# Soft-capped attention and a soft mixture of experts: tanh of three-tile chunks a step ahead of the exp of six tiles, two score buffers, and second-layer loads in pairs of blocks

## The chip, the core and the metric

The kernel runs on one core of a Trainium2 chip. The core has a matrix engine (TensorE, PE), two engines for elementwise work (VectorE, DVE, and ScalarE, ACT, which has the activation functions), a slower general engine (GpSimd, POOL) and a queue engine (SyncE, SP) that mostly starts DMA transfers. Each engine takes its instructions in order, and waits between engines are semaphores. Matmul results go to PSUM, eight banks of 512 fp32 columns on 128 partitions. The metric is the device time of one execution in microseconds (us); lower is better.

## What is computed

Attention has 8 batches, 12 heads, 448 positions and head size 64. The scores are capped by a tanh before the softmax. Its output, reordered to 3584 tokens of 768 features, is the input of a mixture of 8 experts with 4 slots each: every slot is a softmax-weighted mean over all tokens, goes through its expert's two layers, and every token gets back a softmax-weighted mean of the slots.

```python
scores = scale * q @ k.T
scores = cap * tanh(scores / cap)              # cap = 30
attn = softmax(scores, axis=-1)
x = (attn @ v) reordered to [3584, 768]
logits = x @ phi                               # [3584, 32]
d = softmax(logits, axis=0)                    # over tokens
slot_input = (d.T @ x).reshape(8, 4, 768)
for e in range(8):
    slot_out[e] = relu(slot_input[e] @ w1[e]) @ w2[e]     # 768 -> 1024 -> 768
out = softmax(logits, axis=1) @ slot_out       # over slots
```

## The kernel before, in words

**Attention.** Two heads make a pair and two pairs a quad, so there are 24 quads and 48 pairs. A tile is 64 keys of both heads of a pair (128 partitions) by 448 queries; a pair has 7 tiles, and there are 336 in all. The main loop (L402) runs over 84 chunks of four tiles. `qk_chunk` (L215) makes a chunk's transposed scores, two matmuls a tile, in the one score buffer of four PSUM banks. `tanh_chunk` (L227) reads it and writes bf16 to SBUF, which frees the score buffer; `exp_chunk` (L232) runs in place on what tanh has just written. `pv_tile` (L235) multiplies the tile of the chunk before with v, and carries a column of ones in v (so `VW` is 130), by which the row sums of the softmax come out of the same matmul. Two banks (`pv0`, `pv1`) hold the four query groups of a pair. At the last tile DVE takes the reciprocal of the sums and multiplies (L254, L255) into `xq`.

**What runs beside it.** q, k and v come in by SP, a quad at a time; DVE casts q and k (`cast`, L180), PE transposes them through PSUM (`transp`, L188), and DVE copies the result back (L194). POOL casts v into a block layout (`vcast`, L199). For each pair `x_transp` (L263) transposes the attention output, for each quad `logits` (L272) adds its part of the logits, and for each batch `e_exp` (L286) exponentiates them into E, `slot_sums` (L313) adds up the weighted tokens with the sum of E as a seventh column block (by a matrix of ones), and `e_transp` (L290) and `e_sums` (L305) prepare the second softmax. Most of these pass through `psT`, two PSUM banks. The weights are cast in flight by DMAs that POOL starts (L102, L106): all of w1 and the first `R2` = 28 of the 64 blocks of w2 to SBUF, and the rest as bf16 to a scratch in DRAM.

The order is written by hand. `at(j, slot, ...)` puts a piece of work beside chunk `j` in slot "a" or "b", and the loop emits tanh, PV tiles, slot "a", the next scores, slot "b" and exp. Waits come only from data and buffer reuse.

**The tail.** After the last exp come the last PV, transposes, logits, E and slot sums (L416 to L428), with junk matmuls (`busy`) between them. The slot inputs are divided by the sum (L445, L446). The blocks of w2 in the scratch are loaded by SP into the SBUF space that the attention buffers leave, four blocks a DMA (L439); each load waits for the buffers under it. `layer1` (L450) runs four times (two groups of four experts, two halves of 512 features), `h_transp` transposes, and `layer2` (L478) goes through the 64 blocks, both halves of the output columns (384 each) four blocks at a time. The results are cast to `so` (L499, L500), and 28 output tiles follow: two matmuls, a scaling on DVE or ACT by turns (L518, L520), and a store of 384 KB by SP (L521).

## Time and profile before

| | |
|---|---|
| median of 4 runs | 340.54 us (337.99 to 346.36) |
| the profiled execution | 339.12 us, of which 337.3 are the span of the profile |
| first tanh, end of the last exp | 8.08 us, 285.09 us |
| busy: ACT, PE, DVE, POOL | 86%, 75%, 48%, 26% |
| granted PE clock, mean | 0.949 |
| DMA in the span | 76.84 MB, 228 GB/s |

The profile gives each instruction's start and length and what ended the idle time before it. A group's row shows its line, engine, result and sources, shapes and count, then its busy time, the mean of one in ns, and the idle time in front of it. In the windows view a row gives PE, PE's weight loads, DVE, ACT and POOL busy, each with its number of instructions in brackets, then PE's clock (1.00 is full), DMA share and GB/s. In the timeline some matmul records are merged, so that "x28" is one row with the length of all, and a release is named after "<-". "PEld" is PE loading weights, "q" behind an engine's name its queue.

### The profile page before, as it was taken

What the parts mean: (1) busy time and instruction counts of PE and PEld (TensorE: products, weight loads), DVE (VectorE), ACT (ScalarE), POOL (GpSimd) and SP (SyncE); (2) the same over time, 40 slices, a digit from 0 to 9 for tenths busy, and PEclk for the clock granted to TensorE, in tenths of its full rate; (3) what the DMA queues carried; (4) which work ended last, traced back from release to release, by engine and by line L of the source; (5) the groups of instructions that cost most, each with busy time, mean ns of one, the idle gap of its engine ahead of it and who ended that gap; (6) DMA issues with size and microseconds to landing.
All of it is one profiled execution on the core that took longest, in us unless ns stands there. A gap on an engine that the chain in (4) does not pass through costs nothing.

```text
span 337.3 us, 7890 instructions
## 1 busy us (share of the span) xinstructions
PE 252.9 (75%) x3398; PEld 180.8 (54%) x3398; DVE 161.6 (48%) x414; ACT 289.8 (86%) x194; POOL 88.6 (26%) x106
## 2 busy tenths in 40 slices
PE   7668778778687787776787777878877877896670
PEld 6446556555465565564665555556654655553220
DVE  6733545355455453563555354633745433316541
ACT  1999999999999999999999999999999997105450
POOL 3630442145124322540342244313404300000000
PEclk9997997999999899999999999997999999999755
DMA  8977778977987899599779999999899920885997
GB/s 272 255 156 221 177 208 194 221 191 202 188 239 180 174 264 237 172 217 209 204 195 198 273 272 235 244 276 279 192 237 240 230 94 2 315 343 219 398 397 294
DMA packets 40740, 76.84 MB, mean 228 GB/s; under 512 B 3201, under 2 KB 29825, under 8 KB 40705
## 3 DMA queue, kind: packets, MB, share of 16 engines
q1 hardware_dynamic: 24656, 50.67, 43.8%
q0 software_dynamic: 15760, 25.22, 42.8%
q8 instruction: 26, 0.43, 0.5%
q10 hardware_dynamic: 288, 0.46, 0.4%
q14 instruction: 10, 0.07, 0.1%
HBM read 90.54 MB, written 18.09 MB: 322 GB/s over the span
## 4 chain that ended last, share of the span: by engine, by line
ACT 75%; PE 8%; DMA 6%; SPq 3%; DVE 3%; issue 3%; DVEq 0%; ACTq 0%
ACT ex L233 37%; ACT ex L230 37%; DMA w2t<-w2d 4%; SPq L521 3%; PE pv L245 3%; PE sc L224 2%; DMA out_dram<-ob 1%; DMA qraw<-in_q_dram 1%; PE op L514 1%; DVE xq L255 1%; DVE ob L518 1%; ACT E L288 0%; PE xps L267 0%; DVE qT L194 0%; PE slps L321 0%
## 5 line engine op out<-in xcount | busy, mean ns | idle before, releaser
L233 ACT ACTIVATE ex<-ex 128x1792 bf16<-128x1792 bf16 x84 | 142.5, 1696 | 2.4
L230 ACT ACTIVATE ex<-sc 128x1792 bf16<-128x1792 f32 x84 | 138.4, 1647 | 5.7 <-PE sc L224 5.7
L245 PE MATMUL pv<-vbd,ex 128*128 128x130 bf16 x1344 | 101.5, 227 | 28.4 <-ACT ex L233 27.5
L245 PEld LDWEIGHTS <-ex 128*128 128x128 bf16 x1344 | 81.3, 101 | 54.3 <-ACT ex L233 40.2
L224 PE MATMUL sc<-qT,kT 64*64 64x448 bf16 x672 | 71.4, 358 | 31.8 <-ACT ex L230 26.8
L202 POOL CAST vbd<-vraw 64x896 bf16<-64x896 f32 x23 | 21.6, 939 | 174.5 <-PE pv L245 144.9
L224 PEld LDWEIGHTS <-kT 64*64 64x64 bf16 x672 | 35.1, 105 | 44.1 <-issue 27.6
L269 DVE COPY xT<-xps 128x512 bf16<-128x512 bf16 x48 | 20.3, 423 | 56.9 <-PE xps L267 56.8
L255 DVE TENSOR_TENSOR xq<-pv,rec 128x256 bf16<-128x256 f32 x96 | 40.8, 425 | 3.3
L254 DVE RECIPROCAL rec<-pv 128x4 f32<-128x4 f32 x96 | 17.0, 177 | 39.0 <-PE pv L245 39.0
L203 POOL CAST vbd<-vraw 64x896 bf16<-64x896 f32 x23 | 30.8, 1339 | 1.3
L194 DVE COPY qT<-qps 128x896 bf16<-128x896 bf16 x23 | 14.4, 625 | 27.1 <-PE qps L192 27.1
L520 ACT ACTIVATE ob<-op,winv 128x768 f32<-128x768 f32 x14 | 12.5, 901 | 11.3 <-DMA out_dram<-ob 8.5
L514 PE MATMUL op<-so,ET 128*128 128x384 bf16 x56 | 16.8, 400 | 5.7 <-DVE ob L518 3.8
L267 PE MATMUL xps<-ident,xq 128*128 128x128 bf16 x192 | 19.2, 223 | 0.6 <-DVE xq L255 0.6
L518 DVE TENSOR_SCALAR ob<-op,winv 128x768 f32<-128x768 f32 x14 | 14.2, 1017 | 9.8 <-PE op L514 7.4
L102 POOL DMA_DIRECT2D w1b<-in_moe_w_dram x24 | 16.9, 705 | 0.0
L182 DVE CAST qbf<-qraw 128x896 bf16<-128x896 f32 x22 | 14.6, 665 | 0.0
L514 PEld LDWEIGHTS <-ET 128*128 128x128 bf16 x56 | 5.9, 108 | 15.5 <-issue 14.2
L194 DVE COPY kT<-kps 128x896 bf16<-128x896 bf16 x23 | 14.2, 617 | 0.0
L192 PE MATMUL kps<-ident,kbf 128*128 128x128 bf16 x161 | 12.9, 220 | 1.2 <-DVE kbf L182 0.9
L267 PEld LDWEIGHTS <-xq 128*128 128x128 bf16 x192 | 13.1, 100 | 0.9 <-DVE xq L255 0.9
(70 smaller groups left out, 174.8 us busy)
## 6 DMA issues: line engine op xcount, KB each, us to landing
w1b<-in_moe_w_dram POOLq DMA_DIRECT2D x24, 512.0 KB, 8.4
out_dram<-ob SPq DMA_DIRECT2D x28, 384.0 KB, 3.9
vraw<-in_v_dram SPq DMA_DIRECT2D x23, 448.0 KB, 7.3
qraw<-in_q_dram SPq DMA_DIRECT2D x22, 448.0 KB, 3.7
kraw<-in_k_dram SPq DMA_DIRECT2D x22, 448.0 KB, 4.8
w2d<-in_moe_w_dram POOLq DMA_DIRECT2D x9, 768.0 KB, 10.9
w2t<-w2d SPq DMA_DIRECT2D x9, 768.0 KB, 8.0
w2b<-in_moe_w_dram POOLq DMA_DIRECT2D x7, 768.0 KB, 11.4
```

The lines of the kernel that those rows point to most:

```text
L194: dve.tensor_copy(t, ps)
L202: pool.tensor_copy(t[0:HP, :, :, 0:DH], raw[0:HP])
L203: pool.tensor_copy(t[HP:P, :, :, DH + 1:VW - 1], raw[HP:P])
L224: pe.matmul(sc[cs, u, 0:S], qkT["k", Q][r, c, cs], qkT["q", Q][r, :, cs], start=True, stop=True)
L230: act.activation(ex, scores.pop(j)[:, :, 0:S], ACT.Tanh, scale=qk_scale / cap)
L233: act.activation(exs[j], exs[j], ACT.Exp, scale=cap)
L245: pe.matmul(pvs[pr][g // 2][:, g % 2, :], exs[j][:, u, GOFF[g]:GOFF[g] + P], vbds[Q % 2][:, h, c, :], start=(c == 0 and g % 2 == 0), stop= ...
L255: dve.tensor_tensor(xq[Q][:, 2 * s:2 * s + 2, h * P:(h + 1) * P] .rearrange("p g (i d) -> p g i d", i=2), pv[:, :, :, 0:DH], rec.to_broadc ...
L267: pe.transpose(ps[:, g, :], xq[Q][:, g, h * P:(h + 1) * P], ident)
L269: dve.tensor_copy(t, ps)
L514: pe.matmul(op[:, half, 0:HD], et_tile(bb, c), so[half], start=True, stop=True)
L518: dve.tensor_scalar_mul(ob, op[:, :, 0:HD], winv[:, bb, c:c + 1])
```

## The change

The number of tiles for an exp goes from four to six (`CH`), and a chunk of scores becomes three tiles (`CS`) in one of two score buffers. A step of the main loop, of which there are 56, emits tanh of its two half chunks and then exp of the six tiles of the step before; the exp buffers go from three to four. PV runs two steps behind, a pair at a time, in two passes of two query groups (`pv_pass`), each in the one bank of `psV`, with the next scores between them. `psT` has one bank. Four slots ("a" to "d") and one in front ("0") take the other work; one step in seven has no pair and gets 12 junk matmuls. V's cast has its own slots.

At the start, the casts' access pattern gets another dimension, the first copy of kT is made in two parts, and the second half's k goes through `psV`. The sum of E is made by `e_norm` from the copy of E that `e_rep` makes on POOL, and the division moves into the Relu of layer 1, as the scale `rz`.

In the tail, exp of the last chunk is in two parts, the PSUM banks form one pool of seven, and the last pair's transposes, logits and E go in halves. `R2` is 24, the scratch is loaded two blocks a DMA, layer 2 makes all of its first half of columns before the second, and the first halves of five output tiles are made and stored while the second half runs.

```diff
-CH = 4
+CH = 6
+CS = 3
...
-    R2 = 28
+    R2 = 24
...
-    psT = ctx.enter_context(tc.tile_pool(name="psT", bufs=2, space=PSUM))
+    psT = ctx.enter_context(tc.tile_pool(name="psT", bufs=1, space=PSUM))
...
+    ldv = att.enter_context(tc.tile_pool(name="ldv", bufs=1))
+    qk = att.enter_context(tc.tile_pool(name="qk", bufs=2))
     vb = att.enter_context(tc.tile_pool(name="vb", bufs=1))
+    exps = att.enter_context(tc.tile_pool(name="exps", bufs=4))
+    xs = att.enter_context(tc.tile_pool(name="xs", bufs=4))
+    attp = ExitStack()
+    psS = attp.enter_context(tc.tile_pool(name="psS", bufs=2, space=PSUM))
+    psV = attp.enter_context(tc.tile_pool(name="psV", bufs=1, space=PSUM))
...
-                casts[nm, 0][:, :, h * HP:(h + 1) * HP],
-                raws[nm, 0][:, h, :].rearrange("p (c d) -> p c d", d=DH))
+                casts[nm, 0][:, :, h * HP:(h + 1) * HP]
+                .rearrange("p c (a d) -> p a c d", a=2),
+                raws[nm, 0][:, h, :].rearrange("p (c a d) -> p a c d", a=2, d=DH // 2))
...
-            ps = psT.tile([P, NT, P], BF16, name=nm + "ps", tag="T")
+            ps = (psT if nm == "q" else psV).tile(
+                [P, NT, P], BF16, name=nm + "ps", tag="T" if nm == "q" else "pv")
             r = slice(h * HP, h * HP + HP)
             for c in range(NT):
                 pe.transpose(ps[r, c, :], casts[nm, 0][:, c, r], ident)
-            dve.tensor_copy(qkT[nm, 0][r], ps[r])
+            cuts = (0, 2, NT) if (nm, h) == ("k", 0) else (0, NT)
+            for c0, c1 in zip(cuts, cuts[1:]):
+                dve.tensor_copy(qkT[nm, 0][r, c0:c1, :], ps[r, c0:c1, :])
...
+    def qk_chunk(i):
+        sc = psS.tile([P, CS, 512], F32, name="sc", tag="sc")
+        scores[i] = sc
+        for u in range(CS):
+            pr, c = divmod(i * CS + u, NT)
             Q, h = divmod(pr, 2)
             r = slice(h * HP, h * HP + HP)
+            for n in range(2):
+                cs = slice(n * HP, n * HP + HP)
                 pe.matmul(sc[cs, u, 0:S], qkT["k", Q][r, c, cs],
                           qkT["q", Q][r, :, cs], start=True, stop=True)
+    def tanh_chunk(i):
+        j, half = divmod(i, CH // CS)
+        if half == 0:
+            exs[j] = exps.tile([P, CH, S], BF16, name="ex", tag="ex")
+        act.activation(exs[j][:, half * CS:half * CS + CS, :],
+                       scores.pop(i)[:, :, 0:S], ACT.Tanh, scale=qk_scale / cap)
+    def exp_part(j, u0, u1):
+        act.activation(exs[j][:, u0:u1, :], exs[j][:, u0:u1, :], ACT.Exp, scale=cap)
     def exp_chunk(j):
+        exp_part(j, 0, CH)
+    def pv_tiles(pr, half, c0, c1, home=None):
         Q, h = divmod(pr, 2)
+        if c0 == 0:
+            if h == 0 and half == 0:
                 xq[Q] = xs.tile([P, NG, 2 * P], BF16, name="xq", tag="xq")
+            pvs[pr, half] = psV.tile([P, 2, VW], F32, name="pv", tag="pv") \
+                if home is None else home
+        for c in range(c0, c1):
+            j, u = divmod(pr * NT + c, CH)
+            for n in range(2):
+                g = 2 * half + n
+                pe.matmul(pvs[pr, half][:, n, 0:VW],
+                          exs[j][:, u, GOFF[g]:GOFF[g] + P],
+                          vbds[Q % 2][:, h, c, :],
+                          start=(c == 0 and n == 0), stop=(c == NT - 1),
+                          skip_group_check=True)
+    def norm(pr, half):
+        Q, h = divmod(pr, 2)
+        pv = pvs.pop((pr, half))[:, :, 0:VW].rearrange("p g (i w) -> p g i w", i=2)
+        rec = xs.tile([P, 2, 2, 1], F32, name="rec", tag="rec", bufs=4)
+        dve.reciprocal(rec, pv[:, :, :, DH:DH + 1])
+        dve.tensor_tensor(
+            xq[Q][:, 2 * half:2 * half + 2, h * P:(h + 1) * P]
+            .rearrange("p g (i d) -> p g i d", i=2),
+            pv[:, :, :, 0:DH],
+            rec.to_broadcast([P, 2, 2, DH]), op=ALU.mult)
+    def pv_pass(pr, half):
+        pv_tiles(pr, half, 0, NT)
+        norm(pr, half)
...
+    def e_rep(b):
+        e4s[b] = consts.tile([P, NG, 4 * NS], BF16, name="e4", tag="e4", bufs=1)
+        pool.tensor_copy(e4s[b].rearrange("p g (a s) -> p g a s", a=4),
+                         es[b].unsqueeze(2).to_broadcast([P, NG, 4, NS]))
+    def e_norm(b):
+        ps = psT.tile([P, 1], F32, name="zps", tag="T")
+        for g in range(NG):
+            pe.matmul(ps, e4s[b][:, g, :], ones[:, 0:1], start=(g == 0), stop=(g == NG - 1))
+        if b == 0:
+            dve.tensor_copy(zacc, ps)
+        else:
+            dve.tensor_tensor(zacc, ps, zacc, op=ALU.add)
+        if b == B - 1:
+            dve.reciprocal(rz, zacc)
...
+    def slot_mms(b, ps, gs, jts=None):
+        for g in gs:
+            for jt in range(NJ):
+                pe.matmul(ps[:, jt, :],
+                          xq[b * NQB + jt // 2][:, g, (jt % 2) * P:(jt % 2 + 1) * P],
+                          es[b][:, g, :], start=(g == 0 and jt == 0), stop=(g == NG - 1),
+                          skip_group_check=True)
...
+    def spare(n):
+        busy(n, psV.tile([P, 2, VW], F32, name="junk", tag="pv")[:, 0, 0:P])
+    PER = 2 * NQB * NT // CH
+    assert PER == 7 and NQB == 3
+    def quad_in(Q, cast_k, cast_q, k_in, q_in, v_in):
         if 0 < Q < NQ:
             at(*cast_k, cast, "k", Q)
             at(*cast_q, cast, "q", Q)
             at(*k_in, transp, "k", Q)
             at(*q_in, transp, "q", Q)
+            at(*v_in, vcast, Q)
+    for b in range(B):
+        j = b * PER
+        quad_in(3 * b + 1, (j - 1, "d"), (j, "a"), (j, "b"), (j, "c"), (j + 2, "c"))
+        quad_in(3 * b + 2, (j + 1, "c"), (j + 1, "d"), (j + 2, "b"), (j + 2, "c"),
+                (j + 5, "c"))
+        quad_in(3 * b + 3, (j + 3, "d"), (j + 4, "c"), (j + 5, "b"), (j + 5, "c"),
+                (j + 7, "c"))
+        p = 6 * b
+        at(j + 2, "a", spare, 12)
+        at(j + 4, "a", x_transp, p)
+        at(j + 5, "a", x_transp, p + 1)
+        at(j + 6, "a", x_transp, p + 2)
+        at(j + 5, "d", logits, 3 * b)
+        if b < B - 1:
+            at(j + 7, "a", x_transp, p + 3)
+            at(j + 8, "a", x_transp, p + 4)
+            at(j + 7, "d", logits, 3 * b + 1)
+            at(j + 9, "a", x_transp, p + 5)
+            at(j + 9, "d", logits, 3 * b + 2)
+            at(j + 11, "0", e_exp, b)
+            at(j + 11, "d", slot_sums, b)
+            at(j + 12, "d", e_transp, b)
+            at(j + 13, "d", e_norm, b)
+            if b % 2:
+                at(j + 14, "d", e_sums, b // 2)
...
-        at(2 + n * (NCH - 8) // nw, "b", *job)
+        at(1 + n * (NCH - 5) // nw, "b", *job)
...
+    busy(33)
     init_vbd()
     first_half(0)
     qk_chunk(0)
     first_half(1)
+    qk_chunk(1)
+    at(1, "b", vcast, 0)
+    at(3, "b", dve.memset, hpad, 0.0)
     pool.dma_start(out=phib, in_=moe_phi.rearrange("(jt ji) s -> ji jt s", ji=P))
+    def pair_at(j):
+        pr = (j + 1) * CH // NT - 1
+        return pr if pr >= 0 and (pr + 1) * NT > j * CH else None
     for j in range(NCH):
+        run(j, "0")
+        tanh_chunk(2 * j)
+        tanh_chunk(2 * j + 1)
+        if j != 1:
+            exp_chunk(max(j - 1, 0))
+        pr = pair_at(j - 2)
+        if pr is not None:
+            pv_pass(pr, 0)
         run(j, "a")
         if j + 1 < NCH:
+            qk_chunk(2 * j + 2)
         run(j, "b")
+        if pr is not None:
+            pv_pass(pr, 1)
+        run(j, "c")
+        if j + 1 < NCH:
+            qk_chunk(2 * j + 3)
+        run(j, "d")
...
+    exp_part(NCH - 1, 0, CL)
+    exp_part(NCH - 1, CL, CH)
+    attp.close()
+    mid = ExitStack()
+    big = mid.enter_context(tc.tile_pool(name="big", bufs=7, space=PSUM, reuse_waits="tile"))
+    def bank(shape, dt=F32, name="bank"):
+        return big.tile(shape, dt, name=name, tag="b")
+    junk = bank([P, P], name="junk")
+    pv2 = [bank([P, 2, VW], name=f"pvl{half}") for half in range(2)]
+    x_transp(last - 2)
+    for half in range(2):
+        pv = bank([P, 2, VW], name=f"pvm{half}")
+        pv_tiles(last - 1, half, 0, NT, pv)
+        norm(last - 1, half)
+    logits(NQ - 2, bank([P, NG, NS], name="lpl"))
+    for half in range(2):
+        pv_tiles(last, half, 0, NT - CL, pv2[half])
+    x_transp(last - 1)
+    busy(3)
+    for half in range(2):
+        pv_tiles(last, half, NT - CL, NT)
+        norm(last, half)
+    busy(5)
+    xl = xs.tile([P, NG, P], BF16, name="xT", tag="xT", bufs=2)
+    halves = [range(0, 2), range(2, 4)]
+    Q, bl = NQ - 1, B - 1
+    lg, el = lgs.pop(bl), consts.tile([P, NG, NS], BF16, name="E", tag="E", bufs=2)
+    es[bl] = el
+    sl_ps = bank([P, NJ, NS], name="slpl")
+    for s, gs in enumerate(halves):
+        hs = slice(2 * s, 2 * s + 2)
+        ps = bank([P, 2, P], BF16, name="xpl")
+        for g in gs:
+            pe.transpose(ps[:, g - 2 * s, :], xq[Q][:, g, P:2 * P], ident)
+        act.copy(xl[:, hs, :], ps)
+        busy(3)
+    for s, gs in enumerate(halves):
+        hs = slice(2 * s, 2 * s + 2)
+        ps = bank([P, 2, NS], name="lpl")
+        for g in gs:
+            pe.matmul(ps[:, g - 2 * s, :], xTs[2 * Q][:, g, :], phib[:, NJ - 2, :],
+                      start=True, stop=False)
+            pe.matmul(ps[:, g - 2 * s, :], xl[:, g, :], phib[:, NJ - 1, :],
+                      start=False, stop=True)
+        dve.tensor_tensor(lg[:, hs, :], ps, lg[:, hs, :], op=ALU.add)
+        act.activation(el[:, hs, :], lg[:, hs, :], ACT.Exp)
+    busy(5)
+    for gs in halves:
+        slot_mms(bl, sl_ps, gs)
+    for s in range(2):
+        js = slice(3 * s, 3 * s + 3)
+        dve.tensor_tensor(slT[:, js, :], sl_ps[:, js, :], slacc[:, js, :], op=ALU.add)
+    e_rep(bl)
...
-    for n0 in range(R2, len(blocks), 4):
-        t = tl.tile([P, 4, D], BF16, name=f"w2t{n0}")
-        sp.dma_start(out=t, in_=w2d[(n0 - R2) // 4])
+    for n0 in range(R2, len(blocks), 2):
+        t = tl.tile([P, 2, D], BF16, name=f"w2t{n0}")
+        sp.dma_start(out=t, in_=w2d[(n0 - R2) // 4][:, (n0 - R2) % 4:(n0 - R2) % 4 + 2, :])
...
-            act.activation(hbs[i][:, 0:512], hp, ACT.Relu)
+            act.activation(hbs[i][:, 0:512], hp, ACT.Relu, scale=rz)
         else:
-            dve.tensor_scalar_max(hbs[i][:, 512:1024], hp, 0.0)
+            dve.tensor_scalar(hbs[i][:, 512:1024], hp, rz, 0.0, ALU.mult, ALU.max)
...
+    def layer2(n0, half):
+        for n in range(n0, n0 + 4):
+            i, ft, gg = blocks[n]
+            pe.matmul(so_ps[half][32 * gg:32 * gg + NS, :],
+                      hpad[:, 4 * i + gg, ft, :],
+                      w2_block(n)[:, half * HD:(half + 1) * HD],
+                      start=(n0 == 0), stop=(n0 == len(blocks) - 4))
...
+    layer1(0, 0, e_norm)
...
+    def half_tile(n, half, home, eng):
+        if half == 0:
+            obs[n] = wts.tile([P, 2, HD], F32, name="ob", tag="w1", bufs=E)
+        bb, c = divmod(n, NT)
+        pe.matmul(home, et_tile(bb, c), so[half], start=True, stop=True)
+        if eng == "dve":
+            dve.tensor_scalar_mul(obs[n][:, half, :], home, winv[:, bb, c:c + 1])
+        else:
+            act.mul(obs[n][:, half, :], home, winv[:, bb, c:c + 1])
+        store(n, half, half + 1)
...
+    NH = 5
+    so = [wts.tile([P, HD], BF16, name=f"so{half}", tag="w1", bufs=E) for half in range(2)]
+    n2 = len(blocks)
+    for n0 in range(0, n2, 4):
+        if n0 == n2 // 2:
             h_transp(1)
+        layer2(n0, 0)
     act.copy(so[0], so_ps[0])
+    done = 0
+    for n0 in range(0, n2, 4):
+        layer2(n0, 1)
+        if n0 >= 8 and n0 % 8 == 0 and done < NH:
+            half_tile(done, 0, bank([P, HD], name="op0"),
+                      "act" if done % 2 else "dve")
+            done += 1
...
+        if n == NH + 2:
             e_transp(B - 1)
+        if n == NH + 4:
             e_sums(B // 2 - 1)
         op = fin.tile([P, 2, 512], F32, name="op", tag="op")
+        if n < NH:
+            half_tile(n, 1, op[:, 0, 0:HD], "act" if n % 2 else "dve")
+            continue
```

## The prediction

> **What bounds it now.** I read the page's chain and costliest groups first, then ScalarE's (ACT's) timeline, then TensorE (PE) and VectorE (DVE) between two chunks, then the DMA view of the last 67 us.
>
> ```profile
> span 337.3 us, 7890 instructions
> ...
> ACT 75%; PE 8%; DMA 6%; SPq 3%; DVE 3%; issue 3%; DVEq 0%; ACTq 0%
> ...
> L233 ACT ACTIVATE ex<-ex 128x1792 bf16<-128x1792 bf16 x84 | 142.5, 1696 | 2.4
> L230 ACT ACTIVATE ex<-sc 128x1792 bf16<-128x1792 f32 x84 | 138.4, 1647 | 5.7 <-PE sc L224 5.7
> ```
>
> Tanh (L230) and exp (L233) are three quarters of the chain. Of the 5.7 us idle before tanh, 5.14 is the start (first tanh at 8.08), so attention is ACT-bound from 8.08 to 285.09, the end of the last exp. After that: 52.2 us.
>
> The ACT timeline (start, length) shows where two instructions touch:
>
> ```profile
> 49.50 1.70 ACT L233 ACTIVATE ex<-ex 128x1792 bf16<-128x1792 bf16 x1
> 51.11 1.65 ACT L230 ACTIVATE ex<-sc 128x1792 bf16<-128x1792 f32 x1
> 52.78 1.70 ACT L233 ACTIVATE ex<-ex 128x1792 bf16<-128x1792 bf16 x1
> 54.39 1.65 ACT L230 ACTIVATE ex<-sc 128x1792 bf16<-128x1792 f32 x1
> 55.93 0.30 ACT L288 ACTIVATE E<-lg 128x128 bf16<-128x128 f32 x1
> 56.13 1.69 ACT L233 ACTIVATE ex<-ex 128x1792 bf16<-128x1792 bf16 x1
> 57.99 1.66 ACT L230 ACTIVATE ex<-sc 128x1792 bf16<-128x1792 f32 x1 [0.17 <-PE sc L224]
> ```
>
> A tanh starts 1.61 after an exp of 1.70: 0.09 of overlap. The exp that reads what the tanh just wrote starts 1.67 after it, with none, and 0.02 lost. Where E (which reads something else) stands between, tanh and E overlap by 0.11. So the dependence costs about 0.11 a pair, and a pair takes 3.28.
>
> **ScalarE in attention.** The new loop has 56 steps of tanh, tanh (three tiles each) and the exp of six tiles of the step before. The count is unchanged (168 instructions), but only the first exp and the tail's read what the previous instruction wrote. Lengths: between casts of 384 elements (479 ns, L499) and tanh (1647) the slope is 0.83 ns an element; between E (300 ns at 128) and exp (1696) it is 0.84. So tanh of 1344: 1647 - 448 x 0.83 = 1275; exp of 2688: 1696 + 896 x 0.84 = 2448. Step: 2 x 1.275 + 2.448 - 3 x 0.093 = 4.72. 56 x 4.72 = 264.3, plus 0.2 for the first exp and the split last exp: 264.5, against 84 x 3.28 = 275.5. **Gain 11.0.** The Trainium skill, "ScalarE: Activation LUTs", section "What ACT_TABLE_LOAD costs", gives 186 ns + 0.833 a column for any activation with immediates, and 93 ns of overlap back to back. By it a step is 3 x 0.186 + 5376 x 0.000833 - 0.279 = 4.76, and the gain only 275.5 - 266.6 - 0.2 = 8.7. The rows show two fixed costs, not one (0.15 for tanh from PSUM, 0.19 for exp from SBUF), and the change trades exps for tanhs; I take the rows. The eight E cost 0.2 each as before.
>
> **The start.** Casts of 448 take 0.61 (L167); those of 896 with one more loop dimension in their pattern take 0.61 too (L182). The new pattern has that dimension: about 0.38 each, so q and k are ready 0.4 earlier. The kT copy (0.62 for 896) is cut, the first part 256 long (0.28), and the chunk is 6 matmuls, not 8. First tanh near 7.25: **gain 0.8**. If the pattern doesn't help: 0.4. The second tanh waits behind the second half's transposes on PE (about 8.5, when the first ends): nothing.
>
> **What TensorE and VectorE must now hold.** PSUM goes to two score buffers of three banks, and psT and psV fall to one bank. New waits: the second PV half waits for the first's normalization (reciprocal, multiply); every transpose, logit and slot sum waits for the copy of the last user of psT. Behind each of them, in PE's order, stand the next scores that ACT wants.
>
> ```profile
> 99.13 0.94 PE L224 MATMUL sc<-qT,kT 64*64 64x448 bf16 x8 [0.56 <-ACT ex L230]
> 100.01 1.94 PE L245 MATMUL pv<-vbd,ex 128*128 128x130 bf16 x28
> 101.78 0.39 PE L267 MATMUL xps<-ident,xq 128*128 128x128 bf16 x4
> 101.87 0.18 DVE L254 RECIPROCAL rec<-pv 128x4 f32<-128x4 f32 x1 [1.75 <-PE pv L245]
> 102.09 0.42 DVE L255 TENSOR_TENSOR xq<-pv,rec 128x256 bf16<-128x256 f32 x1
> 103.10 0.56 PE L192 MATMUL kps<-ident,kbf 128*128 128x128 bf16 x7
> 103.84 0.62 DVE L194 COPY kT<-kps 128x896 bf16<-128x896 bf16 x1
> ```
>
> PE a batch (7 steps, 33.0 us): 6 pairs x 1.94, 14 half chunks x 0.70, 6 x 0.56, 6 x 0.39, 3 logits x 0.35, slots 0.75, E's transposes, sums and 12 spare matmuls 1.5: 30.3, or 92%. These rows contain each group's drain (28 weight loads of PV take 1.6), so the true need is 25 to 30. A step with both transposes, logits and PV needs 5.2 with drains, over 4.72; the light steps (3.3 without transposes, 2.5 to 3.7 without PV) give it back. Its hand-overs: a normalization takes 0.75 after the half, covered by the 0.70 of scores placed between; a qT copy (0.62) before the logits uncovers about 0.5 behind the last scores of the step. Walking it from tanh's start: first scores end at 2.0 to 2.8, wanted at 4.72; second at 4.7 to 5.4, wanted at 5.9. The next step starts late, and in the one after a heavy one the slack falls to 0 to 0.5. With ex in four buffers, tanh also waits for the first tiles of the previous step's second PV half (at 3.5 to 4.4, wanted by 4.72). So the bound from below is 0, from above 1 us a batch, 8 in all. I take **2.5 lost**, nearer the lower end, since the group rows overstate PE and a late step is made good within two.
>
> The skill's "TensorE: Matmul & The Clock Gate", section "A second HAM failure mode: psum-queue depth-cycling", says that PE idling briefly between groups that cycle through PSUM can make its clock fall back again and again. That speaks against one bank for psT. The trace has such falls:
>
> ```profile
> 30.00:32.00 2.00, 2.00 (x19) 1.31 (x14) 0.18 (x1) 2.00 (x2) 0.00 (x0) 0.50 0.42 72
> ...
> 30.69 3.02 PE L245 MATMUL pv<-vbd,ex 128*128 128x130 bf16 x28
> ```
>
> At clock 0.50 the 28 PV matmuls take 3.02, not 1.94; ACT lost 0.24 after it and 0.17 at 58 us (row above). By windows the clock means 0.95 to 1.00 from 62 to 267, some 14 us at half speed in all attention. The same four falls would each take 1.7 us of PE's work, mostly within slack: they are in the 2.5. By the rule at its worst, the last rival below.
>
> **Queues and edits at nothing.** V casts move to later slots on POOL: a V cast may start when PE leaves the buffer of two quads earlier and is wanted one quad (11.0 us) later; casts 2.3, landing 7.3 (longest 10.1): cover about 8 us, and without it PV would wait for the excess. K and q loads on SP keep their order; they land in 3.3 to 7.6, wanted 8 us later. Weight loads keep their number (40; POOL issue 0.7) and end by about 245. The copy of E to e4 on POOL (0.61) has a step of time. The ones matmuls of the slot sums (4 a batch) become four of the E sums; the scale by 1/z enters the Relu. DVE is 48% busy.
>
> **The tail.**
>
> ```profile
> 286.25 4.90 SPq L439 DMA_DIRECT2D w2t<-w2d  x7
> 304.03 0.51 PE L482 MATMUL so_ps<-w2t,hpad 128*32 128x384 bf16 x8 [1.02 <-DMA w2t<-w2d]
> ...
> GB/s 301 125 21 0 0 0 0 0 0 10 117 374 334 330 422 435 408 411 388 92 0 0 273 396 398 394 398 396 402 394 404 393 400 398 394 396 396 392 347 13
> ...
> out_dram<-ob SPq DMA_DIRECT2D x28, 384.0 KB, 3.9
> ```
>
> Let T be the last exp's end (285.09). Seven w2t loads (5.5 MB) wait for the last PV and land at T+18.9; layer 2 ends behind them; output then flows from T+21.9 at about 395 GB/s for 28 us (11 MB). Both are DMA-bound. Now ten groups come back (R2 = 24: 0.8 MB more) but in 20 pieces, the first eight of which wait only for the last loads, casts and earlier PV, and land before T. Twelve (4.7 MB) wait for the last PV, at about T+1.9 because PV of two pairs queues in front (PE behind by 0.7 to 1). 4.7 MB at 388 GB/s is 12.2: landing at T+16. The slot chain (layer 1 at T+5.2, was 6.35) is hidden by it. Half 0 of layer 2 ends at T+16.1, its cast and first half store put output on at T+18.4: five halves (1 MB, 2.5 us) flow while half 1 (64 matmuls, 2.7) runs. Half 1, cast, scale: the rest flows from T+22.0, a gap of 1.1, for 25.7, and ends at T+47.7 where it was T+50.2. **Gain 2.5**; none if the loads slip by 2.5, 4 if the gap closes. The extra SP issues (0.37) hide under transfers of 0.5.
>
> **Sum.** 337.3 - 11.0 - 0.8 + 2.5 - 2.5 = 325.5. The profiled execution took 339.12, 1.8 over its span: 327.3. That run is 1.4 under the median of the four (340.54), so I put the median at **328.0**.
>
> **Rivals.** (a) The loop is as costed, PE loses nothing: 325 to 326, and 323 with a tail gain of 4. Chance 0.25. (b) As forecast, 326 to 331: 0.43. (c) PSUM hand-overs cost 1 us a batch or more and the tail gives nothing: 328 + 5.5 + 2 = 332 to 336. For it: heavy steps over 4.72; against: each is followed by light ones. 0.19. (d) The overlap isn't got, because a tanh that waits on a semaphore starts afresh; without it for the two tanhs a step is 4.91 and attention 275: 338 to 339.5. Against it: the tanh at 51.11 waits on PE too and overlaps. 0.06. (e) Slower: the single psT and psV banks make PE stall into the slow clock for good. PE's 25 us a batch at half clock is 50, 7.1 a step, 2.4 over ACT's 4.72; six slow steps (40 us, where before had 14) take all the gain, ten give 350. 0.07.
>
> Faster by over 1% 0.87, within 1% (about what a measurement can tell from no change) 0.06, slower 0.07. Range 322.5 to 335: (a), (b) and most of (c).
>
> **What would show it.** ACT: exp rows of 2448, tanh 1275, step 4.72, every neighbour overlapping 0.09. Idle before tanh from PE in steps 1 and 2 of each seven, 2 to 3 us in all. Last exp's end near 275. Last w2t landing 16 us after it, output on by 18.4, the end 49.7 after it. Wrong if PE's clock is low for long stretches, if idle before tanh passes 8, or if POOL waits for V loads and PV for POOL.

## The result, and the profile after

The kernel after the change takes 338.32 us (median; 333.11 to 351.18) where the kernel before takes 340.3 in the same comparison. Executions of one kernel scatter, so the ratio, 0.989 with a 95% interval of 0.986 to 0.991, is taken over those within 1.5% of each kernel's fastest (means 336.1 and 339.9 us), and the profiled execution of the kernel after lies just above that bound. It is 1% faster, not the 3.7% that was forecast, and 338.3 lies outside the range. The profiled execution took 338.42 us, 336.7 of it the span: 11.2 us more than the forecast span (325.5), and these have to be found.

These are rows of the page of the kernel after, in the page's order: the span, the granted clock in 40 slices of 8.4 us, the chain that ended last, and the groups of tanh (L243) and exp (L247).

```profile
span 336.7 us, 8116 instructions
...
PEclk9855999699959999999799959999999699989855
...
ACT 47%; PE 24%; DMA 16%; DVE 8%; issue 2%; SPq 1%; DVEq 0%; ACTq 0%
...
L243 ACT ACTIVATE ex<-sc 128x1344 bf16<-128x1344 f32 x112 | 145.6, 1408 | 14.9 <-PE sc L236 12.0
L247 ACT ACTIVATE ex<-ex 128x2688 bf16<-128x2688 bf16 (+1 forms) x57 | 143.7, 2526 | 0.0
```

ScalarE has fallen from 75% of the chain to 47%; PE, DMA and DVE took its place. In front of tanh ScalarE is idle for 14.9 us, where it was 5.7. Of that, 4.74 is the start (first tanh at 7.68), and 10.1 are stalls inside attention. The last exp ends at 283.56 (forecast 275.8), and the rest takes 53.1 us (forecast 49.7). So 7.8 of the 11.2 us are lost in attention and 3.4 behind it.

The stalls lie in few places: 5.5 us before 36 us, then two each near 61, 96 and 263 us. Ahead of all but the first two (1.61 and 0.23, before 19 us) VectorE waits for a load: 6.76 for k at 21.02, then for q 3.06 at 56.27, 3.00 at 91.30 and 2.01 at 258.22. A fifth wait, 1.41 at 191.51, stalls nothing. This is the timeline of the stall at 96 (start, length; in brackets the idle time before, and what ended it):

```profile
87.69 0.62 DVE L194 CAST kbf<-kraw 128x896 bf16<-128x896 f32 x1
...
88.65 2.55 ACT L243 ACTIVATE ex<-sc 128x1344 bf16<-128x1344 f32 x2
90.07 0.75 PE L236 MATMUL sc<-qT,kT 64*64 64x448 bf16 x6 [1.28 <-ACT ex L243]
90.99 2.54 ACT L247 ACTIVATE ex<-ex 128x2688 bf16<-128x2688 bf16 x1
91.30 0.63 DVE L194 CAST qbf<-qraw 128x896 bf16<-128x896 f32 x1 [3.00 <-DMA qraw<-in_q_dram]
91.85 0.42 DVE L292 COPY xT<-xps 128x512 bf16<-128x512 bf16 x1
...
92.32 0.88 PE L204 MATMUL kps<-ident,kbf 128*128 128x128 bf16 x7 [1.50 <-DVE xT L292]
...
93.32 1.39 ACT L243 ACTIVATE ex<-sc 128x1344 bf16<-128x1344 f32 x1
93.91 0.91 PE L204 MATMUL qps<-ident,qbf 128*128 128x128 bf16 x7 [0.71 <-DVE kT L206]
94.75 1.33 PE L236 MATMUL sc<-qT,kT 64*64 64x448 bf16 x6
...
96.11 1.29 ACT L243 ACTIVATE ex<-sc 128x1344 bf16<-128x1344 f32 x1 [1.41 <-PE sc L236]
96.24 1.68 PE L264 MATMUL pv<-vbd,ex 128*128 128x130 bf16 x14
```

Read it from the wait to the stall. VectorE stands 3.00 us before the q cast, because its load has not landed. Behind the cast, in VectorE's order, stands the copy of `xT`, which frees the one bank of `psT`. So PE's transposes of k wait 1.50 us for that copy. Behind the transposes, in PE's order, stand the second scores of the step, which the tanh at 96.11 wants. This is a "pairless" step, the one in seven without PV, so nothing else on PE fills the time. The windows view (PE, PE's weight loads, DVE, ACT and POOL busy, then the granted clock, DMA share and GB/s) shows what the thin stretch does to the clock:

```profile
88.00:90.00 2.00, 0.79 (x14) 0.71 (x12) 0.31 (x1) 2.00 (x3) 0.00 (x0) 1.00 1.11 257
90.00:92.00 2.00, 0.75 (x6) 0.37 (x6) 0.70 (x2) 2.00 (x3) 0.00 (x0) 1.00 1.08 321
92.00:94.00 2.00, 0.97 (x9) 0.81 (x9) 0.89 (x2) 2.00 (x2) 0.00 (x0) 0.59 0.87 226
94.00:96.00 2.00, 2.00 (x13) 0.91 (x12) 0.62 (x1) 0.71 (x1) 0.81 (x1) 0.50 0.46 171
```

From about 92 us the clock is 0.50: the transposes take 0.88 and 0.91, six scores 1.33 and a half of PV 1.68, where they take 0.55, 0.76 and 0.97 at full clock. From the start of k's transposes to the tanh it is 3.79 us here (92.32 to 96.11), and 2.54 at full clock (58.71 to 61.25 in e1_warm, below). By this estimate the slow clock makes 1.25 of the 1.41 us that the tanh waits.

Why was the load late? SP's queue (issues of the loads):

```profile
82.40 0.37 SPq L153 DMA_DIRECT2D qraw<-in_q_dram  x1
82.86 0.42 SPq L153 DMA_DIRECT2D vraw<-in_v_dram  x1
88.34 0.37 SPq L153 DMA_DIRECT2D kraw<-in_k_dram  x1
91.96 0.37 SPq L153 DMA_DIRECT2D qraw<-in_q_dram  x1
```

The raw q buffer is single, so the load of the next q starts when the cast of the last one has ended: 82.40. VectorE was free for the next q cast at 88.30, 5.9 us later; that cast, which starts when the data are there, came 8.9 us after the issue. The DMA view gives the median from issue to landing, first of the kernel before, then of the one after:

```profile
qraw<-in_q_dram SPq DMA_DIRECT2D x22, 448.0 KB, 3.7
```

```profile
qraw<-in_q_dram SPq DMA_DIRECT2D x22, 448.0 KB, 7.9
```

In the kernel before, the q issued at 80.60 was cast at 92.68, without a wait for its load: 12 us of room for a load of 3.7.

```profile
80.60 0.37 SPq L145 DMA_DIRECT2D qraw<-in_q_dram  x1
92.68 0.62 DVE L182 CAST qbf<-qraw 128x896 bf16<-128x896 f32 x1
```

Why the load itself takes twice as long was not found; it stayed at 7.3 to 7.9 in the faster kernels below (e2, e5 to e7, e9 to e11), too.

### The profile page after: what moved, and what is told of

Read it like the earlier page. It is cut to its first block, busy times and chain, and to the rows that moved or that the text cites. A ratio compares the mean times of both kernels' runs of the same rounds, so it can differ in the third digit from the quotient of the medians.

```text
span 336.7 us, 8116 instructions
## 1 busy us (share of the span) xinstructions
PE 279.4 (83%) x3486; PEld 187.9 (56%) x3486; DVE 172.5 (51%) x426; ACT 282.4 (84%) x199; POOL 83.2 (25%) x107
## 4 chain that ended last, share of the span: by engine, by line
ACT 47%; PE 24%; DMA 16%; DVE 8%; issue 2%; SPq 1%; DVEq 0%; ACTq 0%
ACT ex L247 23%; ACT ex L243 23%; DMA qraw<-in_q_dram 8%; PE pv L264 8%; PE sc L236 5%; DMA kraw<-in_k_dram 3%; DMA out_dram<-ob 2%; DMA w2t<-w2d 2%; PE so_ps L579 1%; PE kps L204 1%; DVE qbf L194 1%; DVE xq L275 1%; PE hp L552 1%; DVE ob L646 1%; PE op L642 1%
## 5 line engine op out<-in xcount | busy, mean ns | idle before, releaser
L243 ACT ACTIVATE ex<-sc 128x1344 bf16<-128x1344 f32 x112 | 145.6, 1408 | 14.9 <-PE sc L236 12.0
L247 ACT ACTIVATE ex<-ex 128x2688 bf16<-128x2688 bf16 (+1 forms) x57 | 143.7, 2526 | 0.0
L264 PEld LDWEIGHTS <-ex 128*128 128x128 bf16 x1344 | 86.0, 104 | 25.1 <-DVE xq L275 17.9
L236 PE MATMUL sc<-qT,kT 64*64 64x448 bf16 x672 | 88.1, 393 | 14.0 <-ACT ex L243 13.4
L214 POOL CAST vbd<-vraw 64x896 bf16<-64x896 f32 x23 | 21.3, 927 | 151.6 <-DMA vraw<-in_v_dram 86.1
L236 PEld LDWEIGHTS <-kT 64*64 64x64 bf16 x672 | 28.9, 111 | 35.5 <-issue 19.4
L215 POOL CAST vbd<-vraw 64x896 bf16<-64x896 f32 x23 | 25.8, 1122 | 1.3
L194 DVE CAST qbf<-qraw 128x896 bf16<-128x896 f32 x22 | 17.6, 801 | 9.5 <-DMA qraw<-in_q_dram 9.5
L292 DVE COPY xT<-xps 128x512 bf16<-128x512 bf16 x47 | 19.5, 415 | 1.0 <-PE xps L290 1.0
L204 PE MATMUL qps<-ident,qbf 128*128 128x128 bf16 x161 | 14.3, 236 | 6.7 <-DVE kT L206 6.7
L204 PEld LDWEIGHTS <-kbf 128*128 128x128 bf16 x161 | 10.7, 100 | 15.9 <-issue 10.4
L194 DVE CAST kbf<-kraw 128x896 bf16<-128x896 f32 x22 | 14.7, 666 | 6.8 <-DMA kraw<-in_k_dram 6.8
L206 DVE COPY qT<-qps 128x896 bf16<-128x896 bf16 x23 | 14.2, 619 | 7.5 <-PE qps L204 7.4
L318 POOL COPY e<-E 128x512 bf16<-128x512 bf16 x8 | 4.9, 617 | 48.8 <-ACT E L312 33.9
```

The lines of the kernel that those rows point to most:

```text
L194: dve.tensor_copy(t.rearrange("p c (h d) -> p h c d", h=2), raws.pop((nm, Q)).rearrange("p h (c d) -> p h c d", d=DH))
L204: pe.transpose(ps[:, c, :], src[:, c, :], ident)
L206: dve.tensor_copy(t, ps)
L214: pool.tensor_copy(t[0:HP, :, :, 0:DH], raw[0:HP])
L215: pool.tensor_copy(t[HP:P, :, :, DH + 1:VW - 1], raw[HP:P])
L236: pe.matmul(sc[cs, u, 0:S], qkT["k", Q][r, c, cs], qkT["q", Q][r, :, cs], start=True, stop=True)
```

## The experiments

Four accounts of the missing time were set against each other. A: PE idles, loses its clock, and ScalarE then waits for a slow PE. B: PE has too much to do with single banks, whatever the loads do. C: the q load lands after its cast's turn, and that alone delays the scores. D, on the tail: its time is set by the order of the halves and the half stores, not by PE's speed. Edits are to the kernel after; where a title names another experiment, the cut shows only what comes on top of that one. Ratios are to the kernel before.

**e1_warm: keep PE busy in the pairless step.**

```diff
         j = b * PER
+        at(j + 2, "b", spare, 40)
```

> Edit: 40 more junk matmuls of 128 columns in front of the k transposes of the step in seven that has no PV (some 2.4 us of PE work a batch, none of it useful). Theory A (an idle PE loses its clock, and ACT then waits for the slow PE): in that step PE no longer stands still for 3 us, its clock stays at 1.00 there, idle before tanh falls from 10.2 us after the start to 4 to 6 (what is left is the start), the last exp ends at 278 to 280 instead of 283.6, ratio to before 0.975 to 0.98. Theory B (PE has too much to do, or hands over its single banks too slowly): more work on PE makes it worse, ACT idles 5 to 15 us more, ratio 1.00 to 1.03. Theory C (the late q load alone delays the scores, whatever the clock): no change, 0.989.

Measured: 342.15 us, ratio 1.001 (0.996 to 1.005). The mean clock is 0.947 (0.886 in the kernel after), and no tanh waits for PV any more. But tanh now waits 0.83 to 0.84 once in each of seven batches, and 3.58 at 27 us. It is the same whether q is late or in time: at 57.65 its cast had waited 3.89, in the batch of 95.25 not at all.

```profile
57.65 0.63 DVE L194 CAST qbf<-qraw 128x896 bf16<-128x896 f32 x1 [3.89 <-DMA qraw<-in_q_dram]
58.71 0.55 PE L204 MATMUL kps<-ident,kbf 128*128 128x128 bf16 x7
61.25 1.29 ACT L243 ACTIVATE ex<-sc 128x1344 bf16<-128x1344 f32 x1 [0.84 <-PE sc L236]
...
95.25 1.29 ACT L243 ACTIVATE ex<-sc 128x1344 bf16<-128x1344 f32 x1 [0.83 <-PE sc L236]
```

So the clock can be held, and the waits for PV were a consequence of its fall. At full clock a late q load adds nothing to what the 40 matmuls in front of the scores cost by themselves, and that is more than they save.

**e2_late_casts: cast and transpose later.** The quad that falls on the pairless step is cast and transposed up to one step later, so its load has more time and its transposes stand behind other scores; one more quad's k cast moves back as well.

```diff
-        quad_in(3 * b + 2, (j + 1, "c"), (j + 1, "d"), (j + 2, "b"), (j + 2, "c"),
+        quad_in(3 * b + 2, (j + 2, "a"), (j + 2, "b"), (j + 3, "a"), (j + 3, "b"),
                 (j + 5, "c"))
-        quad_in(3 * b + 3, (j + 3, "d"), (j + 4, "c"), (j + 5, "b"), (j + 5, "c"),
+        quad_in(3 * b + 3, (j + 4, "b"), (j + 4, "c"), (j + 5, "b"), (j + 5, "c"),
```

> Edit: the casts of the second and third quad of a batch come 0.75 to 1.25 steps later, and the second quad's transposes move into the next step, so that three casts of k (and of q) lie 10.5 to 11 us apart instead of 8 to 14. Theory C: DVE no longer waits for the q loads (16.3 us before), the scores are never late, and idle before tanh falls to that of the start: last exp at 278 to 280, ratio 0.975 to 0.98. Theory A: DVE's wait goes too, but the step without PV has now two transposes less (1.1 us), PE is still idle in it, the clock still falls in some batches and ACT still idles there: idle 6 to 10 us, ratio 0.98 to 0.99. Theory B: the work is spread more evenly, idle 4 to 6.

Measured: 329.14 us, ratio 0.963 (0.956 to 0.970). The last exp ends at 273.35, and after 17.2 us ScalarE does not stall once. The chain of this kernel:

```profile
ACT 80%; DMA 6%; PE 6%; SPq 3%; DVE 2%; issue 1%; DVEq 0%; ACTq 0%
...
L243 ACT ACTIVATE ex<-sc 128x1344 bf16<-128x1344 f32 x112 | 155.0, 1588 | 5.5 <-PE sc L236 5.5
```

Nothing but the place of casts and transposes was changed: PE's work, its single banks and the number of transfers are the same. B falls. The ratio is lower than A and C forecast. And it is not that the loads are in time now: VectorE still waits 11.8 us for k and q (6.6 and 5.2), where it waited 16.3 in the kernel after. Which of the two moves did it, e6 and e7 take apart.

**e3_start: the second score chunk ahead of the second half of quad 0.**

```diff
+    qk_chunk(1)
     first_half(1)
-    qk_chunk(1)
```

> Edit: the scores of tiles 3 to 5 are emitted before the second half's transposes. All theories: the second tanh follows the first without the 1.61 us of idle. If nothing behind takes it up, the run is 1.6 us shorter, ratio 0.984. Rival: the third step waits for the k load that lands at 21.0 us in any case (2.63 us of idle at 25.6), which takes most of the gain back: ratio 0.988, idle at the third step 4 us.

Measured: 340.16 us, ratio 0.989 (0.982 to 0.995). The second tanh's wait of 1.61 is gone, but in its place came one of 2.25 at 16 us, behind k transposes whose cast took 1.35 us, and one of 1.84 is left at 25 us, behind a k cast that waited 5.45 for its load. The ratio is that of the kernel after, so nothing is gained. (The last exp ends at 286.56, 3.0 later, with stalls in later batches that this edit does not touch.)

**e4_tail_warm: junk matmuls ahead of each of the loaded groups in half 0 of layer 2.**

```diff
+    wjunk = bank([P, P], name="wjunk")
...
             h_transp(1)
+        if n0 >= R2:
+            busy(6, wjunk)
         layer2(n0, 0)
```

> Edit: six junk matmuls in front of each group of four blocks of the first half of layer 2 whose weights come from the scratch (they fill PE's waits for the loads). Theory A: the clock stays at 1.00 through the second half, which takes 3.5 us instead of 6.3, the output flows in full 2.5 us earlier, from last exp to the end 50.5 us instead of 53.1, ratio 0.981. Rival D: the stores of half tiles and the gap behind them set the end, not PE: 0 to 1 us, ratio 0.986 to 0.989.

Measured: 336.56 us, ratio 0.985 (0.976 to 0.993). The windows at the same place in half 1, of the kernel after and then of this one:

```profile
302.00:304.00 2.00, 2.00 (x16) 0.48 (x18) 0.62 (x1) 0.00 (x0) 0.00 (x0) 0.50 0.00 0
```

```profile
300.00:302.00 2.00, 1.91 (x31) 0.55 (x27) 0.62 (x1) 0.83 (x2) 0.00 (x0) 1.00 0.00 0
```

At full clock, 31 matmuls run in 2 us where 16 did, and from the cast of half 0 to that of half 1 it takes 4.7 us instead of 5.7. But the junk stood in the chain of half 0, which ended 2 us later, so the tail is 54.9, not shorter. Nor was it needed: the same distance is 4.7 to 4.8 in the six other experiments with half tiles (e1 to e3, e6 to e8), so the slow half 1 belongs to the one execution of the kernel after. The last exp is at 280.01 in this run, with 6.7 us of stalls after the first tanh where there were 10.1, and the edit cannot touch that: the stalls in attention differ from run to run by a few us.

**e5_late_nohalf: e2_late_casts without half output tiles.**

```diff
-    NH = 5
+    NH = 0
```

> The loads' casts as late as in e2_late_casts, and no half output tiles in layer 2 (each output tile is computed whole after both halves, as the kernel before does). My forecast's tail theory (half tiles computed and stored early are worth about 2.5 us): slower than e2_late_casts' 0.963 by 2.5 us, a ratio near 0.970. Theory D (half 1 of layer 2 runs its half tiles inside its own chain, 5.0 us in e2 where 24 bare groups would need some 2.7, and the stores cannot use the early start, since the output comes at full rate only 4 us later): the tail is unchanged within 0.5 us, ratio 0.961 to 0.965.

Measured: 329.72 us, ratio 0.967 (0.961 to 0.974); last exp 273.47, tail 54.5 against e2_late_casts' 51.8. D fell in this part: between these two traces the half stores are worth 2.8 us, close to the forecast's 2.5. The ratios differ by 0.005 in the same direction, inside their intervals, and tails with half tiles run from 51.5 (e8) to 54.2 (e1); the table below has a steadier measure.

**e6_transp_later: only the transposes later.** The casts stay where the change has them.

```diff
-        quad_in(3 * b + 2, (j + 1, "c"), (j + 1, "d"), (j + 2, "b"), (j + 2, "c"),
+        quad_in(3 * b + 2, (j + 1, "c"), (j + 1, "d"), (j + 3, "a"), (j + 3, "b"),
```

> The changed kernel, with only the transposes of each batch's pairless-step quad moved one step later in TensorE's order; the casts stay where they are, so VectorE still waits for the q load. If the stall comes from TensorE's order (transposes that wait for a cast stand in front of score chunks), the batch stalls go but VectorE's wait stays: last exp at about 274 us, ratio near 0.965. If it is VectorE's order (the q cast, waiting for its load, stands in front of the copy of xT and with it of everything that needs the psT bank), the stalls stay: ratio about 0.989 as the changed kernel.

Measured: 327.78 us, ratio 0.963 (0.957 to 0.969); last exp 273.30. VectorE still waits for late loads. The views of what engines wait for (total, times, longest), of VectorE here:

```profile
DVE kbf L194 <- DMA kraw<-in_k_dram: 7.8, 2, 6.4
...
DVE qbf L194 <- DMA qraw<-in_q_dram: 3.5, 2, 2.9
```

and of PE, first in the kernel after and then here:

```profile
PE kps L204 <- DVE xT L292: 5.6, 11, 1.5
```

```profile
PE kps L204 <- DVE xT L292: 0.2, 1, 0.2
```

So VectorE may wait 6 us for a load without harm, as long as PE does not. What stalled ScalarE is PE's order: transposes that depend on the load stood in front of scores that did not. This is a late q load here; the scores run before its cast, at half clock (1.33), and the tanh follows the exp without a gap:

```profile
116.96 2.69 ACT L247 ACTIVATE ex<-ex 128x2688 bf16<-128x2688 bf16 x1
117.36 1.33 PE L236 MATMUL sc<-qT,kT 64*64 64x448 bf16 x6 [0.43 <-ACT ex L243]
117.63 0.63 DVE L194 CAST qbf<-qraw 128x896 bf16<-128x896 f32 x1 [2.89 <-DMA qraw<-in_q_dram]
...
119.30 2.71 ACT L243 ACTIVATE ex<-sc 128x1344 bf16<-128x1344 f32 x2
```

The clock still dips elsewhere, too (the row of slices, below), also without harm.

```profile
PEclk9769997899999979997899999978998997999855
```

Not all of the 10.3 us by which the last exp is earlier than in the profile of the kernel after is the edit's: 1.2 of them lie before 20 us, where nothing has moved yet. By the ratios the edit is worth 2.6% (0.989 to 0.963).

**e7_q_early: q one quad earlier.** Two raw buffers for q; R2 is 20 to make room. Casts and transposes stay where the change has them.

```diff
-    R2 = 24
+    R2 = 20
...
-                                               tag=nm + "raw")
+                                               tag=nm + "raw", bufs=2 if nm == "q" else 1)
...
-        if Q > 1:
+        if nm == "q":
+            load(nm, Q + 2)
+        elif Q > 1:
             load(nm, Q + 1)
```

> The changed kernel with two buffers for raw q, so that q of the next-but-one quad is loaded one quad earlier; its casts and transposes stay where they are. Four fewer weight blocks are held (R2 20), so two more pair loads fall in the tail, which may cost it up to 2 us. Theory C (the q load that lands after its cast's turn is the root of the batch stalls): VectorE's wait for q is gone, the clock stays up in the pairless steps, only the start's stalls (k, at 21 to 30 us) remain; last exp 278 to 279, end about 331 to 333, ratio 0.972 to 0.978. Theory B (TensorE has too much to do with one psT bank, whatever the loads do): the batch stalls stay, last exp 283 or later, ratio 0.989 or above.

Measured: 334.28 us, ratio 0.981 (0.975 to 0.988); last exp 279.31. VectorE's wait for q in the loop is gone, and with it every wait for scores after 26 us. The timeline at the same place as above:

```profile
87.94 0.37 SPq L153 DMA_DIRECT2D qraw<-in_q_dram  x1
...
88.92 0.56 PE L206 MATMUL kps<-ident,kbf 128*128 128x128 bf16 x7
...
90.20 0.55 PE L206 MATMUL qps<-ident,qbf 128*128 128x128 bf16 x7 [0.71 <-DVE kT L208]
90.68 0.76 PE L238 MATMUL sc<-qT,kT 64*64 64x448 bf16 x6
91.51 2.55 ACT L245 ACTIVATE ex<-sc 128x1344 bf16<-128x1344 f32 x2
```

Transposes 0.56, scores 0.76, and two tanhs without a gap. Left are the start (5.2 us of stalls up to 30 us, where one k load is still late) and three waits for PV of 0.3 to 0.4. The clock still falls: it is at 0.50 from 58 to 66 us, with no wait for scores, because the transposes had run before. C holds in that the load in time takes the stalls for scores away, with 4.25 us (283.56 to 279.31); that the late load alone makes them is not shown (the clock, below); the other 6.0 us between here and e6_transp_later lie mostly in the start. The ratio lies above the forecast's 0.972 to 0.978, which its interval reaches.

**e8_warm16: e1_warm with 16 matmuls.**

```diff
         j = b * PER
+        at(j + 2, "b", spare, 16)
```

> 16 extra matmuls in the pairless step in place of e1_warm's 40. Theory A (TensorE idle loses its clock, and the slow scores and products behind it are the stall): keeping it warm with less work removes most of the batch idle and not the start's; last exp 279 to 280, ratio about 0.975 to 0.978. If the wait for the q load alone makes the stall, whatever the clock, or 16 are too few to bridge 3 us of waiting (16 x 54 ns = 0.9 us), it reads as the changed kernel, 0.987 to 0.990.

Measured: 336.78 us (333.26 to 342.37), ratio 0.986 (0.981 to 0.992). In the profiled execution the last exp is at 280.57: one wait for PV is left, and waits for scores of 0.7 to 1.6 in four batches. The median does not tell it from the kernel after. Each of these waits lies in or just behind a stretch at half clock (0.50 over 86 to 88 us, before a wait of 0.70 at 90.53), and after 40 us the clock falls in no batch but these. Only one of the four, 1.59 at 125.28, follows a late q cast (3.41 at 121.00). So 16 matmuls do not hold the clock, and where it falls tanh waits, as A says; but here the 16 stand in front of the scores as well, so how much is the clock's and how much theirs this run can't say.

**e9_oldtail: e6_transp_later with the second layer in the order of the kernel before.** Both halves side by side, the loop over half 1 gone, and no half tiles.

```diff
-    NH = 5
+    NH = 0
...
     for n0 in range(0, n2, 4):
-        if n0 == n2 // 2:
+        if n0 == 16:
             h_transp(1)
-        layer2(n0, 0)
+        for half in range(2):
+            layer2(n0, half)
     act.copy(so[0], so_ps[0])
...
```

> e6_transp_later's attention, with the second layer in the order of the kernel before (both halves of so_ps side by side, block group by block group, no half output tiles); the loads in pairs stay. Forecast's tail theory (halves one after the other, with stored half tiles, are worth 2.5 us): tail about 54.5 us as in e5_late_nohalf, ratio near 0.967. Theory D (the halves' order gives nothing: the second half ends 4 to 5 us after the first, and what the half tiles store early only pays that back): both halves ready about 18.5 us after the last exp (w2t's last landing at 17.2, and four matmuls of 0.33), then 32.7 us to the end as before: tail 51.2 to 51.6, ratio 0.956 to 0.960.

Measured: 325.52 us, ratio 0.955 (0.949 to 0.962); last exp 273.09, tail 50.4, even shorter than D said. (The ratio of e6 is 0.963, and the intervals overlap; the tails below are the firmer reading.) The rows of the two casts that end layer 2, of the kernel after and then of this one (length least/median/most, then first and last start):

```profile
L618 ACT CAST so<-so_ps x1: 479/479/479, 301.4 to 301.4; 128x384 bf16<-128x384 f32 x1
L626 DVE CAST so<-so_ps x1: 557/557/557, 307.1 to 307.1; 128x384 bf16<-128x384 f32 x1
```

```profile
L619 ACT CAST so<-so_ps x1: 479/479/479, 290.8 to 290.8; 128x384 bf16<-128x384 f32 x1
L620 DVE CAST so<-so_ps x1: 558/558/558, 291.0 to 291.0; 128x384 bf16<-128x384 f32 x1
```

Counted from the last exp, the two casts, the first store's issue and the end are:

| kernel | half 0 | half 1 | first store | end |
|---|---|---|---|---|
| before | 19.3 | 19.5 | 21.4 | 52.2 |
| after | 17.8 | 23.5 | 19.8 | 53.1 |
| e2_late_casts | 17.6 | 22.3 | 19.1 | 51.8 |
| e5_late_nohalf | 17.8 | 21.8 | 23.8 | 54.5 |
| e6_transp_later | 19.0 | 23.8 | 20.6 | 53.3 |
| e9_oldtail | 17.7 | 17.9 | 19.8 | 50.4 |
| e10_oldtail_fours | 17.3 | 17.4 | 19.4 | 49.9 |

From half 1 to the end it is 32.7 us without half tiles (before, e5; 32.5 in e9) and 29.5 with them (e2, e6): they do store 3 us' worth early. But half 0 is no earlier alone than both halves together, since both wait for the last weights, and half 1 follows 4 to 5.7 us later.

**e10_oldtail_fours: e9_oldtail with loads in groups of four.**

```diff
-    for n0 in range(R2, len(blocks), 2):
+    for n0 in range(R2, len(blocks), 4):
...
-        return w2b[:, n, :] if n < R2 else w2t[(n - R2) // 2][:, (n - R2) % 2, :]
+        return w2b[:, n, :] if n < R2 else w2t[(n - R2) // 4][:, (n - R2) % 4, :]
```

> e9_oldtail with the second-layer weights loaded in groups of four blocks, as the kernel before does. If the loads in pairs matter, the last group's eight matmuls of 0.33 us lie behind its landing where the pair has four: tail 1.3 us longer than e9_oldtail's. If the transfers' own rate sets the last landing and TensorE has the time, the tails agree within 0.4 us.

Measured: 324.76 us, ratio 0.954 (0.946 to 0.962), tail 49.9. Loads in pairs bring nothing in this order.

**e11_best_start: e9_oldtail with the edit of e3_start.**

> e9_oldtail with the second score chunk ahead of the second half of quad 0 (the edit of e3_start). There it took away the second tanh's wait, and what it gained went into waits at the k transposes behind it; with those transposes moved back the gain should stay: 0.8 to 1.1 us off e9_oldtail's last exp (273.3), ratio 0.953 to 0.958. The rival: the chunks behind it wait in its place again and nothing is gained.

Measured: 324.99 us, ratio 0.954 (0.948 to 0.961). Last exp 273.01, 0.1 earlier than without: the second tanh's wait (0.95 at 9.3 us) is gone, and a new one of 0.76 stands at 14.2. The rival was right, and the start is worth nothing here. e9 to e11 cannot be told apart; each is some 4.5% faster than the kernel before and 3.4% faster than the one after (0.955 over 0.989).

## Why the prediction was wrong

- **ScalarE's step: right, and a little better than forecast.** Exps follow each other every 4.68 us where no E stands between, against 4.72 forecast. From e2_late_casts' ScalarE timeline:

```profile
41.73 2.53 ACT L247 ACTIVATE ex<-ex 128x2688 bf16<-128x2688 bf16 x1
44.07 2.55 ACT L243 ACTIVATE ex<-sc 128x1344 bf16<-128x1344 f32 x2
46.41 2.54 ACT L247 ACTIVATE ex<-ex 128x2688 bf16<-128x2688 bf16 x1
```

  The lengths are those forecast (1.29 and 2.44 in the first steps); the overlaps are 0.11 to 0.12, not 0.093. Less the stalls, it took 265.8 us from the first tanh to the end of the last exp in the kernel after, and 264.9 in e2, where the forecast has 266.1 (264.5 and eight E of 0.2). So the step gave 0.3 to 1.2 us more than forecast. The rows came nearer than the Trainium skill's figure in "ScalarE: Activation LUTs", "What ACT_TABLE_LOAD costs" (4.76). Rival (d), no overlap, is out, although 338.3 lies in its range.
- **The start: half of it in this run, and by a race.** First tanh at 7.68 (forecast 7.25). The first half's casts did fall to 0.39 each, as forecast, but those of the second half took 1.13, while POOL cast v, and the second tanh, costed at nothing, waited 1.61. In e6, whose code is the same up to there, these casts came just ahead of POOL's and took 0.37 and 0.38; its first tanh is at 6.99, and the second waits 0.29.
- **PE's hand-overs: the step that failed.** 2.5 us were taken for the single banks, with 8 as the upper bound; the stalls were 10.1, and the forecast's own sign of being wrong, "if idle before tanh passes 8", came true. The banks were not at fault (e2 and e6 keep them, with 1.2 and 1.4 us of stalls after the first tanh). What failed is one sentence under "edits at nothing": "K and q loads on SP keep their order; they land in 3.3 to 7.6, wanted 8 us later." The first figure was the kernel before's, and the second stands there without a working. In the trace the q buffer came free late, after a cast of 1.20 beside POOL's, so there were 5.9 us for a load of 8.9. With it failed "the light steps give it back": the lightest step is the one in which PE waits on that load and has nothing else to do. The walk over PE's step counted work and banks, and left out that the transposes wait for a transfer.
- **The clock: the warning was right, the size was not.** The forecast had four falls "mostly within slack", and rival (e) let PE's full banks bring them on. The mean clock in attention was 0.90, for 0.98 in the kernel before, and the fall at 92 us came in the emptiest step, after two gaps of 1.3 and 1.5 us, where the late transposes had used up the slack. By the estimate above (2.54 us from k's transposes to the tanh at full clock) the slow clock makes some 3.9 us of the waits for scores at 26, 61, 96 and 263 us. With the 2.8 of waits for PV, which are gone where the clock is held (e1), that is two thirds of the 10.1. The slow clock alone isn't enough: with the transposes behind the scores (e6 at 117 us) or done in time (e7 at 58), the same half clock makes no tanh wait for scores. And a late load whose transposes run at full clock costs little: in the kernel after, the q wait of 1.41 at 191.51 stalled nothing.
- **The tail: one term right, one mis-sized.** Layer 1 began at T+4.7 (forecast 5.2), half 0's cast at T+17.8 (16.1), and the half stores are worth 3 us (2.5). The landing at T+16 holds 1.9 us that its sum, 1.9 and 12.2, does not name; the last block landed at T+17.3. Half 1 was forecast at "64 matmuls, 2.7"; from cast to cast it measured 4.0 bare (e5), 4.7 with the half tiles (e2) and 5.7 at the clock of the kernel after. So the rest flowed at full rate from T+26.4, not T+22.0. Against the kernel before, half 1's matmuls were moved from under the loads to behind them. And the order of before, with an earlier layer 1, would have given the forecast's 49.7 without any half tile: e10 has 49.9.
- **The sum.** Stalls of 10.1 for 2.5, a start 0.4 later and ScalarE 0.3 better make, within 0.1, the 7.8 us in attention; with 3.4 in the tail that is the 11.2. (The forecast's 328.0 is less than its own 327.3 and 1.4.) With the transposes one step later (e6) the kernel runs in 327.8, which is the forecast, but by luck, since two misses cancel: its last exp is 2.5 us earlier (273.3 for 275.8), its tail 3.6 longer (53.3 for 49.7).

## What to carry to other kernels

When a change moves the steps of a loop, give every single-buffered load its own line in the sum: the shortest time from the release of its buffer to its next use, against the longest landing that the trace shows, with room to spare (the forecast's longest was 7.6 us, and 8.9 came). Work that waits for a transfer belongs behind, not in front of, the work that the bounding engine wants next, and most of all in steps that look light. Splitting a stage so that its first half ends early pays only if the second half is hidden as well as it was before.

## What the hardware showed that was not expected

- **The clock falls without a long gap, and stays down for 3.4 us or a multiple.** Before 92 us PE had two gaps of 1.28 and 1.50 with 0.75 of scores between, and the clock fell; it was back only after 102 us, though PE shows busy for 2.00 of every 2 us from 94 on. By the windows (0.59 over 92 to 94, 0.50 to 102, 0.85 over 102 to 104) that is 10.2 us at half speed. In e6 the windows from 116 to 122 (0.84, 0.50, 0.80) give 3.4, and the kernel after shows 6.8 at 58 and 3.4 at 160. The Trainium skill ("TensorE: Matmul & The Clock Gate", "What's actually happening") gives one window of some 3.4 us for either way. The lengths agree with one, two and three such windows. What it doesn't say is that 0.75 us of scores in the 3.4 us before the fall can pass for idle, or why the return took three windows.
- **VectorE's casts beside POOL's.** The casts of 448 elements took 0.39 with POOL idle and 1.13 beside its v cast; the q cast of 896 took 1.20 instead of 0.62 at 81.17 us, with a v cast from 80.94 to 81.89. In e6 the two casts of 448 that came before POOL's took 0.37 and 0.38. That is seen in the timelines, and was not tested apart.
- **An activation's recorded length is not its cost.** In e2_late_casts the mean exp is recorded with 2.71 us and tanh with 1.59, in e6_transp_later with 2.55 and 1.42, and both end attention within 0.05 us of each other. The distance between starts stayed 4.68; only the recorded overlap grew.
